# Attention and mixture of experts on one core: the products with v in two groups of six heads, the rows of a tile in one step of their own

## The chip, the cores and the metric

The kernel runs on one core of a Trainium2 chip. The metric is the device time of one execution in microseconds (us). Three runs of the kernel before took 1297.36, 1302.81 and 1301.54 us, so its median is 1301.54 us. One execution was profiled; every row below comes from it.

## The reference

For 8 batches of 448 queries with 12 heads of 64, scores are mixed over the heads before the softmax and the probabilities are mixed over the heads again after it. The attended rows (3584 tokens of 768) then go each to the best of 8 experts.

```python
scores = scale * np.matmul(q, k.transpose(0, 1, 3, 2))
scores = np.einsum('bhij,hg->bgij', scores, w_pre)
attn = np.exp(scores - max); attn /= attn.sum(-1) + 1e-9
attn = np.einsum('bhij,hg->bgij', attn, w_post)
x = np.matmul(attn, v)                    # (8, 12, 448, 64) -> (3584, 768)
expert_idx = np.argmax(x @ w_gate, axis=1)
out[token] = gate * (np.maximum(x[token] @ w1[e], 0) @ w2[e])
```

## The kernel before, in words

The attention part cuts the queries of a batch into four tiles, three of 120 queries and one of 88, so that there are 32 tiles T. A tile is worked off in steps of twenty queries (two halves of ten): six steps for a tile of 120, numbered 0 to 5 here, and five for the tile of 88, the last with one half. A batch thus has 23 steps, and the whole attention part 184.

Every step does the same softmax work on TensorE, VectorE, ScalarE and GpSimd:

- `mix` (L267, or L261 for a single half) multiplies the scores of the step with the first head mixing into two banks of PSUM, `bm`.
- `maxima` (L273, VectorE) and `powers` (L281, ScalarE) read those banks: the maximum, then the exponential and its sum. `recip` (L289, L291, VectorE) and `weigh` (L298, GpSimd) make the second mixing, divided by the sums, in the next step.
- `post` (L314) multiplies the exponentials of two steps ago with it into two banks `bp`, and `evict_p` (L332, VectorE; L326 for a single half) copies them into `pt`, the probabilities of the tile, transposed. Both banks are used by every step, so that `post` of a step needs `evict_p` of the step before.

Beside it, some steps carry work that is done once per tile. In steps 0, 2 and 4, `qk` (L239) makes the scores of four heads for a tile to come, in the four banks `bs`, and `evict_s` (L244, ScalarE) copies them out; these are the qk steps. In the others stands the product with v of the tile before: `av` (L346) for a group g of four heads (sixteen products of 64 columns, of two heads side by side, over four pieces of the keys) into the first bank of `bs`; `evict_x` (L353, VectorE) copies it into `xt`; in a later step without `qk`, `rows` (L363) turns it into rows by two products with the matrix `xg` (an identity with eight columns of the gate beside it), and `evict_r` (L370, ScalarE) copies these into `xr`. When three groups are through, `store_x` writes the rows to memory by a DMA of SyncE, and the routing follows: `choose` (L385 to L396, VectorE) finds the expert, `rank` (L404, TensorE) and `place` (L417 to L426, VectorE) its slot, `gate` (ScalarE) and `token` (L432 to L436, VectorE) the weight, and `scatter` (L442), an indirect DMA that GpSimd issues, writes slot and weight into a table.

After step 184 come the last products with v and the last routing, and then the experts: 8 times two layers of matmuls, that begin when the table and the rows have been read back.

No scheduler decides the order. `at(u, stage, ...)` puts a piece of work into step u, `ORDER` gives the order of the stages within a step, and each engine executes what it gets in that order; semaphores make it wait. For a tile of six steps the three groups of `av` of the tile before stand in steps 3, 5 and 1 of the next tile, and each group's `rows` one or two steps behind. In the tile of five steps the second group stands in step 4, which has `qk` too.

Of the kernel before, what the change touches and what calls it, by code (L numbers as in the profile page):

```python
# [8 lines left out]
F32 = mybir.dt.float32  # L9
# [10 lines left out]
B, H, S, D = 8, 12, 448, 64  # L20
# [3 lines left out]
P = 128  # L24
IT = 120
# [9 lines left out]
XG = P + NE  # L35
NTILE = B * 4
# [6 lines left out]
def attn_moe_kernel(ctx, tc, qT, kT, v, w_pre, w_post, w_gate, w1, w2, out):  # L43
    nc = tc.nc
# [291 lines left out]

    HOME = {g: bank_s[0][:, 0, :] for g in range(3)}
    SHEET = {}

    def av(T, g):  # L340
        b, it, ni = geom[T][:3]
        for p in range(2):
            for c in range(NJ):
                for r in range(2):
                    h = 4 * g + 2 * p + r
                    nc.tensor.matmul(out=HOME[g][r * D:(r + 1) * D, p * IT:p * IT + ni],  # L346
                                     lhsT=VV[b][:, c, h * D:(h + 1) * D],
                                     rhs=PT[T][:, c, h, :ni], start=(c == 0), stop=(c == NJ - 1))

    def evict_x(T, g):  # L350
        ni = geom[T][2]
        XT[T, g] = x_p.tile([P, 2, IT], F32, name="xt", bufs=3)
        nc.vector.tensor_copy(out=XT[T, g][:, :, :ni],  # L353
                              in_=HOME[g][:, :2 * IT].rearrange("p (c i) -> p c i", i=IT)[:, :, :ni])

    XR, LG, DD = {}, {}, {}

    def rows(T, g, bank):
        ni = geom[T][2]
        xt = XT.pop((T, g))  # L360
        SHEET[T, g] = bank[:, :2 * XG].rearrange("p (c x) -> p c x", x=XG)
        for c in range(2):
            nc.tensor.matmul(out=SHEET[T, g][:ni, c, :], lhsT=xt[:, c, :ni],  # L363
                             rhs=xg[:, 2 * g + c, :], start=True, stop=True)

    def evict_r(T, g):
        ni = geom[T][2]
        if g == 0:
            XR[T] = x_p.tile([IT, NPAIR, XG], F32, name="xr", bufs=2)
        nc.scalar.copy(out=XR[T][:ni, 2 * g:2 * g + 2, :], in_=SHEET.pop((T, g))[:ni])  # L370

# [10 lines left out]
    def choose(T):  # L382
        b, it, ni = geom[T][:3]
        lg = sm_p.tile([IT, NE], F32, name="lgs")
        nc.vector.reduce_sum(out=lg[:ni], in_=XR.pop(T)[:ni, :, P:XG].rearrange("p c e -> p e c"),  # L385
                             axis=AX.X)
# [102 lines left out]
    def at(u, stage, *what):  # L489
        steps.setdefault((u, stage), []).append(what)  # L490
# [11 lines left out]

    qsteps, vsteps = {}, {}
    for T in range(NTILE):
        u0, n = ustart[T], len(geom[T][3])
        for g, (dt, k) in enumerate(((2, 4), (1, 0), (1, 2))):
            if T + dt < NTILE:
                qsteps[T + dt, g] = u0 + k
        if T + 1 == NTILE:
            vsteps.update({(T - 1, g): u0 + 2 + g for g in range(3)})  # L510
            vsteps.update({(T, g): NU + 1 for g in range(3)})
            vsteps[T - 2, 2] = u0 + 1
        else:
# [3 lines left out]
    hasq = set(qsteps.values())  # L517

    def free(u):
        while u in hasq:  # L520
            u += 1
        return u

    used = {}
    for T in range(NTILE):
        b, it, ni = geom[T][:3]
        u0, n = ustart[T], len(geom[T][3])
        last = T + 1 == NTILE
        if T > 1:
# [15 lines left out]
        if last:  # L545
            continue
        for g in range(3):
            u = vsteps[T, g]
            at(u, "av", av, T, g)
            both = u in hasq  # L550
            at(u if both else u + 1, "vec_now" if both else "vec", evict_x, T, g)
            u = free(u + 1)
            bank = bank_s[1][:, used.get(u, 0), :]
            used[u] = used.get(u, 0) + 1
            at(u, "rows", rows, T, g, bank)
            at(u + 1, "evict_r", evict_r, T, g)
        at(u + 2, "store", store_x, T)
        at(u + 2, "vec", choose, T)
        u = free(u + 3) if T + 3 < NTILE else u + 2
# [35 lines left out]
    for u in range(max(u for u, _ in steps) + 1):  # L595
# [7 lines left out]
        if u == NU + 1:  # L603
            T = NTILE - 1
            HOME.update({0: bank_s[0][:, 0, :], 1: bank_s[0][:, 1, :], 2: bank_s[1][:, 0, :]})
            for g in range(3):
                av(T, g)
                evict_x(T, g)
                if g:
                    rows(T, g - 1, bank_m[g - 1])  # L610
                    evict_r(T, g - 1)
            rows(T, 2, bank_s[1][:, 1, :])
            evict_r(T, 2)
    store_x(T)
# [273 lines left out]
```

## Time and profile before

| | |
|---|---|
| median of three runs | 1301.54 us |
| the profiled execution's own time | 1301.47 us |
| its span, first to last instruction | 1299.8 us |
| TensorE busy | 1234.3 us, 95% |
| VectorE, ScalarE, GpSimd busy | 61%, 52%, 29% |
| attention part (first product with v of tile 0 to the last) | 57.6 to 731.5 us |
| one batch, step 2 of its first tile to the same step a batch later | 86.9 us |

The attention part is a little over half of the span. Durations of matmuls in the trace are modelled and overlap each other, so that what a group of matmuls costs is read from starts: from its first start to the first start of the next group.

### The profile page before, as it was taken

The page shows a single profiled execution, that of the slowest core. Times are in us where ns is not written, and L with a number is a line of the kernel's source. Part 1 is how long each engine was busy: PE and PEld are TensorE (multiplying, and loading weights), DVE is VectorE, ACT ScalarE, POOL GpSimd, SP SyncE. Part 2 cuts the span into 40 slices and gives each one's busy share as a digit, 9 for nine tenths or more (in the row PEclk, how much of TensorE's full clock was granted, in tenths as well). Part 3 has the DMA queues.
Part 4 walks back from the last instruction along what each step waited for, and adds up shares of the span by engine and source line. Part 5 has one row for each costly group of instructions (what it writes and reads, how often), then busy time and mean ns, then how long its engine had stood idle before and what let it go on. Part 6 is the DMA issues. An engine that isn't in the chain of part 4 may idle for free. (4 is left out here: it accounts for less than half of the span.)

```text
span 1299.8 us, 45032 instructions
## 1 busy us (share of the span) xinstructions
PE 1234.3 (95%) x18960; PEld 1032.0 (79%) x18960; DVE 787.9 (61%) x1995; ACT 679.0 (52%) x1468; POOL 371.8 (29%) x605
## 2 busy tenths in 40 slices
PE   6899999999999999999999469999999999999995
PEld 3677777777777777777777459898999989989995
DVE  4777887878878878788788535352434243534320
ACT  5676777767767777777674224242423242434220
POOL 4444453534434535344332120101010202010000
PEclk9999999999999999999999769999999999999998
DMA  6654746746547367566344354443444434544210
GB/s 210 195 164 142 246 123 190 210 151 204 178 136 241 125 192 213 155 201 182 130 153 134 82 178 156 145 159 122 138 140 151 131 133 142 171 135 145 87 36 33
DMA packets 133214, 200.08 MB, mean 154 GB/s; under 512 B 40002, under 2 KB 110674, under 8 KB 132996
## 3 DMA queue, kind: packets, MB, share of 16 engines
q1 hardware_dynamic: 125888, 173.08, 42.5%
q0 software_dynamic: 6064, 23.86, 5.3%
q8 instruction: 161, 2.64, 0.9%
q14 instruction: 57, 0.47, 0.1%
q10 hardware_dynamic: 1044, 0.04, 0.0%
HBM read 97.59 MB, written 23.06 MB: 93 GB/s over the span
## 5 line engine op out<-in xcount | busy, mean ns | idle before, releaser
L281 ACT ACTIVATE et<-bm,st 124x448 f32<-124x448 f32 x360 | 225.5, 632 | 139.9 <-DVE st L273 137.4
L273 DVE TENSOR_REDUCE st<-bm 124x1 f32<-124x448 f32 x360 | 208.1, 619 | 90.3 <-PE bm L267 85.7
L314 PEld LDWEIGHTS bp<-wp,et 60*64 60x64 f32 (+1 forms) x10080 | 199.8, 135 | 71.2 <-issue 48.7
L298 POOL TENSOR_SCALAR wp<-Wpost,st 124x60 f32<-124x60 f32 x360 | 151.4, 435 | 280.7 <-DVE st L291 145.2
L332 DVE COPY pt<-bp 128x480 f32<-128x480 f32 x352 | 213.8, 649 | 26.0 <-PE bp L314 25.7
L314 PE MATMUL bp<-wp,et 60*64 60x60 f32 (+1 forms) x10080 | 193.4, 219 | 1.7 <-issue 1.5
L267 PE MATMUL bm<-sb,Wquad 60*60 60x448 f32 (+3 forms) x1408 | 188.3, 566 | 5.9 <-ACT et L281 4.5
L346 PE MATMUL bs<-pt,vt 128*64 128x120 f32 (+1 forms) x3072 | 173.5, 265 | 2.5 <-DVE pt L326 1.4
L244 ACT COPY si<-bs 120x896 f32<-120x896 f32 (+1 forms) x188 | 160.8, 910 | 26.4 <-PE bs L239 25.4
L346 PEld LDWEIGHTS bs<-pt,vt 128*64 128x64 f32 x3072 | 151.5, 138 | 9.1 <-issue 2.0
L738 POOL DMA_INDIRECT out<-y,ti x30 | 30.0, 1000 | 424.3 <-ACT y L736 415.1
L708 PE MATMUL pm_h<-xh,ah 128*128 128x512 f32 (+1 forms) x384 | 146.1, 381 | 1.8 <-ACTq L767 1.5
L708 PE MATMUL pm_h<-xl,ah 128*128 128x512 f32 (+1 forms) x384 | 146.0, 380 | 0.0
L708 PE MATMUL pm_h<-xh,al 128*128 128x512 f32 (+1 forms) x384 | 144.7, 377 | 0.0
L712 DVE SCALAR_TENSOR_TENSOR hl<-pm_h,hh 128x512 fp32r<-128x512 f32 (+1 forms) x64 | 42.2, 659 | 158.1 <-ACT hh L711 158.1
L711 ACT ACTIVATE hh<-pm_h 128x512 fp32r<-128x512 f32 (+1 forms) x64 | 36.7, 573 | 174.1 <-PE pm_h L708 169.6
L729 PE MATMUL pm_y<-bh,hh 128*128 128x384 f32 x480 | 124.7, 341 | 0.0
L729 PE MATMUL pm_y<-bh,hl 128*128 128x384 f32 x480 | 122.4, 336 | 0.0
L729 PE MATMUL pm_y<-bl,hh 128*128 128x384 f32 x480 | 122.3, 336 | 0.0
L142 POOL TENSOR_TENSOR ql<-qr,qh 128x360 fp32r<-128x360 f32 (+1 forms) x78 | 69.1, 896 | 125.1 <-ACT qh L141 93.1
L736 ACT ACTIVATE y<-pm_y,tb 128x384 f32<-128x384 f32 x30 | 17.5, 582 | 146.3 <-PE pm_y L729 88.0
L239 PE MATMUL bs<-kh,qh 64*120 64x448 f32 (+1 forms) x384 | 82.0, 423 | 12.2 <-ACT kh L115 7.3
(113 smaller groups left out, 1809.2 us busy)
## 6 DMA issues: line engine op xcount, KB each, us to landing
sb<-si SPq DMA_DIRECT2D x344, 210.0 KB
wraw<-in_w SPq DMA_DIRECT2D x48, 512.0 KB
wraw<-in_w SPq DMA_DIRECT2D x64, 384.0 KB
kr<-in_kT SPq DMA_DIRECT2D x42, 224.0 KB
vt<-in_v SPq DMA_DIRECT2D x8, 1152.0 KB
qr<-in_qT SPq DMA_DIRECT2D x48, 180.0 KB
XD<-xr SPq DMA_DIRECT2D x24, 360.0 KB
vt<-in_v SPq DMA_DIRECT2D x16, 192.0 KB
```

The costliest lines, as they stand in the source:

```text
L142: (nc.vector if T == 0 else nc.gpsimd).tensor_sub(out=lo, in0=src, in1=hi.bitcast(F32))
L239: nc.tensor.matmul(out=bank_s[c % 2][:ni, r, :S], lhsT=qx[hs, c, :ni], rhs=kx[hs, :], start=(n == 0), stop=(n == 2))
L244: copy(out=SI[T][:ni, 2 * c:2 * c + 2, :], in_=bank_s[c % 2][:ni, :, :S])
L267: nc.tensor.matmul(out=bank_m[r][CUT[c], :S], lhsT=Wquad[CUT[r], CUT[c]], rhs=sb[CUT[r], c, :], start=True, stop=True)
L273: nc.vector.reduce_max(out=st[:R1, 0, c:c + 1], in_=bank_m[c][:R1, :S], axis=AX.X, negate=True)
L281: nc.scalar.activation(out=et[:R1, c, :], in_=bank_m[c][:R1, :S], func=AF.Exp, bias=st[:R1, 0, c:c + 1], scale=1.0, accum_out=st[:R1, 1, c ...
L298: nc.gpsimd.tensor_scalar(out=wp[:R1, c, :], in0=Wpost[:R1], scalar1=st[:R1, 2, c:c + 1], scalar2=None, op0=ALU.mult)
L314: nc.tensor.matmul(out=bank_p[r][col * JC:(col + 1) * JC, at_:at_ + W], lhsT=et[CUT[r], n, kg * JC:(kg + 1) * JC], rhs=wp[CUT[r], n, :], s ...
L332: nc.vector.tensor_copy(out=flat[:, :, i0 + r * IB:i0 + (r + 1) * IB] .rearrange("p x (n k) -> p x n k", k=IQ), in_=bank_p[r][:, :2 * NJ * ...
L346: nc.tensor.matmul(out=HOME[g][r * D:(r + 1) * D, p * IT:p * IT + ni], lhsT=VV[b][:, c, h * D:(h + 1) * D], rhs=PT[T][:, c, h, :ni], start ...
L708: nc.tensor.matmul(out=ph[:, :n], lhsT=wx[:, fs], rhs=xx[:, kt, :n], start=(m == 0), stop=(m == 3 * NK1 - 1))
L729: nc.tensor.matmul(out=py[g][:, :384], lhsT=hx[:, kt, ts], rhs=wx[:, g * 384:(g + 1) * 384], start=(n == 0), stop=(n == 3 * NK2 - 1))
```

## The change

The product with v of a tile is done in two groups of six heads instead of three of four. A group has 24 products instead of sixteen, and its home is three columns of pairs wide instead of two. The two groups stand in steps 3 and 5 of the next tile, each without `rows` behind it; where that tile has five steps, both stand in step 3, in two banks. The rows of the tile are made in one step of their own, step 1 of the tile after that one: six products in a row, in two banks, copied out by ScalarE in two pieces at the head of step 2. `evict_x` and `evict_r` run twice per tile, on 360 and 408 columns instead of 240 and 272. The number of products is the same.

The routing moves with it. `choose` stands in step 3 behind `evict_p` instead of at the head of a step, `rank` and `gate` stand in step 1 of the tile after, `place` in step 2, `token` behind `evict_p` of step 3, and `scatter` in step 4, behind that step's `weigh`. At the end of the attention part the same pieces stand closer.

```diff
-    def av(T, g):
+    def av(T, g, bank):
         b, it, ni = geom[T][:3]
-        for p in range(2):
+        HOME[T, g] = bank[:, :3 * IT].rearrange("p (c i) -> p c i", i=IT)[:, :, :ni]
+        for p in range(3):
             for c in range(NJ):
                 for r in range(2):
-                    h = 4 * g + 2 * p + r
+                    h = 6 * g + 2 * p + r
...
     def rows(T, g, bank):
-        for c in range(2):
+        for c in range(3):
...
-            for g, (dt, k) in enumerate(((1, 3), (1, n - 1), (2, 1))):
-                if T >= dt:
-                    vsteps[T - dt, g] = u0 + k
+        if T:
+            early = T + 1 == NTILE
+            vsteps[T - 1] = (u0 + 2, u0 + 3) if early else (u0 + 3, u0 + (5 if n > 5 else 3))
+            rsteps[T - 1] = u0 + 4 if early else u0 + n + 1
...
+        for g in range(2):
+            at(vs[g], "av", av, T, g, bank_s[0][:, g if vs[0] == vs[1] else 0, :])
+            at(vs[g] + 1, "vec", evict_x, T, g)
+            at(r, "rows", rows, T, g, bank_s[1][:, g, :])
+            at(r + 1, "evict_r", evict_r, T, g)
+        near = T + 2 - NTILE
+        at(r + 2, "store", store_x, T)
+        at(r + (1 if near == 0 else 2), "choose", choose, T)
+        u = r + 2 if near == 0 else r + 3 if near == -1 else rsteps[T + 1]
         at(u, "rank", rank, T)
         at(u, "gate", gate, T)
         at(u + 1, "vec", place, T)
-        at(u + 2, "vec", token, T)
-        at(u + 2, "scatter", scatter, T)
+        at(u + (1 if near > -2 else 2), "token", token, T)
+        at(u + (2 if near > -2 else 3), "scatter", scatter, T)
...
-             "vec_now", "qk", "evict_s", "split", "split_w")
+             "choose", "token", "qk", "evict_s", "split", "split_w")
```

TensorE, steps 1 and 3 of a tile of six steps (the difference of the two orders; `bp` is written by `post`, `bm` by `mix`, and a row with x16 stands for sixteen products in a row):

```order
 L314 MATMUL bp_106<-wp,et 64x60 x2
-L346 MATMUL bs_101<-pt,vt 64x120 x16
-L363 MATMUL bs_102<-xg,xt 120x136 x2
+L362 MATMUL bs_102<-xg,xt 120x136 x6
 L267 MATMUL bm_103<-sb_150,Wquad 64x448
...
 L314 MATMUL bp_106<-wp,et 64x60 x2
-L346 MATMUL bs_101<-pt,vt 64x120 x16
-L363 MATMUL bs_102<-xg,xt 120x136 x2
+L346 MATMUL bs_101<-pt,vt 64x120 x24
 L267 MATMUL bm_103<-sb_148,Wquad 64x448
```

Each of these steps had a group of `av` and a group of `rows` between `post` and the next `mix`; now it has one of the two, and a longer one.

TensorE, steps 3 and 4 of the tile of five steps:

```order
-L346 MATMUL bs_101<-pt,vt 64x120 x16
-L363 MATMUL bs_102<-xg,xt 120x136 x2
+L346 MATMUL bs_101<-pt,vt 64x120 x48
 L261 MATMUL bm_103<-sb_150,Wpre 124x448
...
 L314 MATMUL bp_106<-wp,et 64x60 x2
-L346 MATMUL bs_101<-pt,vt 64x120 x16
 L239 MATMUL bs_101<-kh,qh 120x448 x2
```

All 48 products of the tile before now stand in step 3, and step 4 has `qk` directly behind `post`.

VectorE, the end of a step and the head of the next around `choose`, before:

```order
L332 COPY pt<-bp_106 128x48x10
L289 TENSOR_SCALAR st<-st 124x2
L291 RECIPROCAL st<-st 124x2
L385 TENSOR_REDUCE lgs<-xr 120x8
...
L396 TENSOR_SCALAR sc<-m_2110 120x1
L273 TENSOR_REDUCE st<-bm_103 124x1
```

and now (steps 3 and 4):

```order
L332 COPY pt<-bp_106 128x48x10
L384 TENSOR_REDUCE lgs<-xr 120x8
...
L395 TENSOR_SCALAR sc<-m_2916 120x1
L431 TENSOR_SCALAR sc<-sc 88x1
L434 RECIPROCAL tg<-sc 88x1
L435 COPY tg<-tokid 88x1
L289 TENSOR_SCALAR st<-st 124x2
L291 RECIPROCAL st<-st 124x2
L353 COPY xt<-bs_101 128x360
L273 TENSOR_REDUCE st<-bm_103 124x1
```

The six lines of `choose` and the three of `token` stand ahead of `recip` and `evict_x` of the next step, where `choose` stood behind `recip`.

## Rows read from the trace of the kernel before

**Rows 1.** The page: busy time of each engine, and TensorE's granted clock in forty slices of the span (tenths of full speed).

```profile
PE 1234.3 (95%) x18960; PEld 1032.0 (79%) x18960; DVE 787.9 (61%) x1995; ACT 679.0 (52%) x1468; POOL 371.8 (29%) x605
PEclk9999999999999999999999769999999999999998
```

**Rows 2.** Waits of TensorE between 40 and 860 us, two of eleven: line and what it waited for, us in total, times, longest.

```profile
PE pm_x L661 <- DMA xs<-XD,tcl: 16.1, 1, 16.1
...
PE bs L239 <- DVE st L289: 3.6, 7, 0.5
```

**Rows 3.** Two stretches of one batch (four tiles) each: length, then busy us of PE, PEld, DVE, ACT and POOL with their instructions, granted clock, share of the DMA engines, GB/s.

```profile
205.27:292.41 87.14, 86.42 (x2023) 67.41 (x2022) 70.45 (x210) 63.45 (x150) 38.63 (x66) 1.00 0.58 178
...
379.33:466.22 86.89, 86.31 (x2024) 67.46 (x2023) 70.48 (x210) 63.44 (x150) 38.67 (x66) 1.00 0.57 181
```

**Rows 4.** TensorE in order of time, around three groups of `av` and `rows`: start us, length us, line, operation, records (one product has two).

```profile
202.37 1.86 PE L346 MATMUL bs<-pt,vt 128*64 128x120 f32 x32
204.16 1.19 PE L363 MATMUL bs<-xg,xt 128*120 128x136 f32 x8
205.27 0.98 PE L267 MATMUL bm<-sb,Wquad 64*64 64x448 f32 x8
206.08 0.99 PE L314 MATMUL bp<-wp,et 64*64 64x60 f32 x56
206.99 0.47 PE L239 MATMUL bs<-kh,qh 64*120 64x448 f32 x2
...
210.21 1.77 PE L346 MATMUL bs<-pt,vt 128*64 128x88 f32 x32
211.91 0.72 PE L363 MATMUL bs<-xg,xt 128*120 128x136 f32 x4
212.56 0.98 PE L267 MATMUL bm<-sb,Wquad 64*64 64x448 f32 x8
...
224.79 1.43 PE L346 MATMUL bs<-pt,vt 128*64 128x88 f32 x32
226.15 0.70 PE L363 MATMUL bs<-xg,xt 128*88 128x136 f32 x4
```

**Rows 5.** TensorE in step 4 of the tile of five steps: `av` and, behind it, `qk` (in brackets the idle time before it, and what ended that).

```profile
106.80 1.86 PE L346 MATMUL bs<-pt,vt 128*64 128x120 f32 x32
109.17 0.46 PE L239 MATMUL bs<-kh,qh 64*120 64x448 f32 x2 [0.51 <-DVE st L289]
```

**Rows 6.** The turn from a qk step to a step 5 (which begins with the row of PE): VectorE, and `mix` of TensorE.

```profile
302.11 1.21 DVE L332 COPY pt<-bp 128x480 f32<-128x480 f32 x2
303.24 0.16 DVE L289 TENSOR_SCALAR st<-st 124x2 f32<-124x2 f32 x1
...
303.51 0.22 DVE L385 TENSOR_REDUCE lgs<-xr 120x8 f32<-120x48 f32 x1
...
304.64 1.15 DVE L273 TENSOR_REDUCE st<-bm 124x1 f32<-124x448 f32 x2
...
302.82 1.29 PE L267 MATMUL bm<-sb,Wquad 64*64 64x448 f32 x8
```

**Rows 7.** All engines in a step 3, which begins with the first row: the scatter and what stands beside it.

```profile
295.55 1.06 PE L267 MATMUL bm<-sb,Wquad 64*64 64x448 f32 x8
295.73 0.16 DVE L289 TENSOR_SCALAR st<-st 124x2 f32<-124x2 f32 x1
...
296.00 0.13 DVE L432 TENSOR_SCALAR sc<-sc 120x1 f32<-120x1 f32 x1
...
296.25 0.13 DVE L436 COPY tg<-tokid 120x1 int32<-120x1 int32 x1
296.28 0.84 POOL L298 TENSOR_SCALAR wp<-Wpost,st 124x60 f32<-124x60 f32 x2 [2.18 <-DVE sc L432]
...
297.29 1.05 POOL L442 DMA_INDIRECT TB<-tg,di  x1 [0.18 <-DVE st L273]
297.34 0.96 PEld L346 LDWEIGHTS bs<-pt,vt 128*64 128x64 f32 x24
...
298.55 0.38 PEld L346 LDWEIGHTS bs<-pt,vt 128*64 128x64 f32 x8 [0.25 <-issue]
...
298.62 1.22 DVE L332 COPY pt<-bp 128x480 f32<-128x480 f32 x2 [0.80 <-PE bp L314]
```

**Rows 8.** TensorE and GpSimd at the end of the attention part, where a scatter stands beside `post`.

```profile
705.86 0.85 PE L314 MATMUL bp<-wp,et 64*64 64x60 f32 x43
...
706.35 1.04 POOL L442 DMA_INDIRECT TB<-tg,di  x1 [0.18 <-issue]
...
707.58 0.39 PE L314 MATMUL bp<-wp,et 60*64 60x60 f32 x9 [0.39 <-issue]
707.89 1.86 PE L346 MATMUL bs<-pt,vt 128*64 128x120 f32 x32
```

**Rows 9.** The copy of a group's products by VectorE, between 60 and 700 us: count, busy us, mean ns of one, idle before.

```profile
L353 DVE COPY xt<-bs 128x240 f32<-128x240 f32 x67 | 26.4, 393 | 4.2 <-PE bs L346 4.0
```

**Rows 10.** ScalarE at the turn from step 1 to step 2.

```profile
291.23 0.82 ACT L141 CAST qh<-qr 128x360 fp32r<-128x360 f32 x1
292.52 0.68 ACT L370 COPY xr<-bs 120x272 f32<-120x272 f32 x2 [0.47 <-PE bs L363]
294.24 0.64 ACT L281 ACTIVATE et<-bm,st 124x448 f32<-124x448 f32 x1 [1.05 <-DVE st L273]
```

More of the change, by code (lines that the diff above doesn't have):

```diff
@@ L335, in evict_p @@
                 in_=bank_p[r][:, :2 * NJ * W].rearrange("p (n x k) -> p x n k", n=2, k=IQ))
-    HOME = {g: bank_s[0][:, 0, :] for g in range(3)}
-    SHEET = {}
-    def av(T, g):
+    HOME, SHEET = {}, {}
+    def av(T, g, bank):
         b, it, ni = geom[T][:3]
-        for p in range(2):
+        HOME[T, g] = bank[:, :3 * IT].rearrange("p (c i) -> p c i", i=IT)[:, :, :ni]
+        for p in range(3):
             for c in range(NJ):
                 for r in range(2):
-                    h = 4 * g + 2 * p + r
-                    nc.tensor.matmul(out=HOME[g][r * D:(r + 1) * D, p * IT:p * IT + ni],
+                    h = 6 * g + 2 * p + r
+                    nc.tensor.matmul(out=HOME[T, g][r * D:(r + 1) * D, p, :],
                                      lhsT=VV[b][:, c, h * D:(h + 1) * D],
@@ L351, in evict_x @@
         ni = geom[T][2]
-        XT[T, g] = x_p.tile([P, 2, IT], F32, name="xt", bufs=3)
-        nc.vector.tensor_copy(out=XT[T, g][:, :, :ni],
-                              in_=HOME[g][:, :2 * IT].rearrange("p (c i) -> p c i", i=IT)[:, :, :ni])
+        XT[T, g] = x_p.tile([P, 3, IT], F32, name="xt", bufs=2)
+        nc.vector.tensor_copy(out=XT[T, g][:, :, :ni], in_=HOME.pop((T, g)))
     XR, LG, DD = {}, {}, {}
@@ L360, in rows @@
         xt = XT.pop((T, g))
-        SHEET[T, g] = bank[:, :2 * XG].rearrange("p (c x) -> p c x", x=XG)
-        for c in range(2):
-            nc.tensor.matmul(out=SHEET[T, g][:ni, c, :], lhsT=xt[:, c, :ni],
-                             rhs=xg[:, 2 * g + c, :], start=True, stop=True)
+        SHEET[T, g] = bank[:, :3 * XG].rearrange("p (c x) -> p c x", x=XG)[:ni]
+        for c in range(3):
+            nc.tensor.matmul(out=SHEET[T, g][:, c, :], lhsT=xt[:, c, :ni],
+                             rhs=xg[:, 3 * g + c, :], start=True, stop=True)
     def evict_r(T, g):
@@ L369, in evict_r @@
             XR[T] = x_p.tile([IT, NPAIR, XG], F32, name="xr", bufs=2)
-        nc.scalar.copy(out=XR[T][:ni, 2 * g:2 * g + 2, :], in_=SHEET.pop((T, g))[:ni])
+        nc.scalar.copy(out=XR[T][:ni, 3 * g:3 * g + 3, :], in_=SHEET.pop((T, g)))
     def store_x(T):
@@ L384, in choose @@
         lg = sm_p.tile([IT, NE], F32, name="lgs")
-        nc.vector.reduce_sum(out=lg[:ni], in_=XR.pop(T)[:ni, :, P:XG].rearrange("p c e -> p e c"),
+        nc.vector.reduce_sum(out=lg[:ni], in_=XR[T][:ni, :, P:XG].rearrange("p c e -> p e c"),
                              axis=AX.X)
@@ L500, in attn_moe_kernel @@
         at(u + PL, "evict_p", evict_p, T, s)
-    qsteps, vsteps = {}, {}
+    qsteps, vsteps, rsteps = {}, {}, {}
     for T in range(NTILE):
@@ L527, in attn_moe_kernel @@
         u0, n = ustart[T], len(geom[T][3])
-        last = T + 1 == NTILE
         if T > 1:
@@ L544, in attn_moe_kernel @@
                 at(U - 15 + 2 * c, "early", split_k, b + 1, c)
-        if last:
+        if T + 1 == NTILE:
             continue
[L547 to L559, printed above, removed]
+        vs, r = vsteps[T], rsteps[T]
+        for g in range(2):
[7 more added lines that the diff above has]
+        u = r + 2 if near == 0 else r + 3 if near == -1 else rsteps[T + 1]
         at(u, "rank", rank, T)
@@ L604, in attn_moe_kernel @@
             T = NTILE - 1
-            HOME.update({0: bank_s[0][:, 0, :], 1: bank_s[0][:, 1, :], 2: bank_s[1][:, 0, :]})
-            for g in range(3):
-                av(T, g)
+            for g in range(2):
+                av(T, g, bank_s[g][:, 0, :])
                 evict_x(T, g)
[L609 to L613, printed above, removed]
+            for g in range(2):
+                rows(T, g, bank_m[g])
+                evict_r(T, g)
     store_x(T)
```

11 lines of the change are left out of this document (removed).

## The prediction, made before the changed kernel was run

> **What bounds the kernel now.** I read the page first, for the busy shares: TensorE is busy for 95% of the span, the other engines for 29 to 61%, and the clock is granted nearly everywhere but at the turn to the experts [rows 1]. Second the waits of TensorE, to see whether the busy share hides a wait. Beside one wait of 16.1 us for the first rows of the experts, none of them sums to more than a few microseconds; the one that this change touches is `qk` waiting seven times for about 0.5 us on VectorE [rows 2]. Third the stretches of one batch: 86.9 to 87.1 us, TensorE busy for all but 0.6 of them, VectorE for 70.5 and ScalarE for 63.5, at full clock [rows 3]. So in the attention part TensorE is the pacer, and what a group of products costs is the distance from its first start to the next group's [rows 4]. What changes those distances changes the time; what VectorE and ScalarE save is worth nothing as long as they keep up. The experts are untouched.
>
> **The change part by part.** The number of products stays; what changes is how often TensorE goes from one kind to another.
>
> *Rows.* A group of two products takes 211.91 to 212.56 = 0.65 us, one of four takes 204.16 to 205.27 = 1.11 [rows 4]. A further two cost 0.46, so 0.19 of each group is its turn in and out. A batch has twelve groups of two, of which two stand together (the row with x8): eleven turns. Four groups of six are left: 7 x 0.19 = 1.33 us less per batch.
>
> *Products with v.* Sixteen of them take 202.37 to 204.16 = 1.79 us with 120 columns and 224.79 to 226.15 = 1.36 with 88 [rows 4]. They run as eight pairs, so 32 columns are 0.43 / 8 = 0.053 us, 120 columns 0.20, and eight pairs 1.60: again 0.19 for the turn. A batch goes from twelve turns to seven (two groups for three tiles; in the tile of five steps both stand in a row): 5 x 0.19 = 0.95 us less. What this rests on is that `rows` behind `post`, which the trace does not show, has the same turn as behind `av`. It could be none or, at most, the 0.19 of `av` on top of its own; from the rows I take them alike.
>
> *The step with both av and qk.* There `av` to `qk` is 106.80 to 109.17 = 2.37 us instead of 1.79: `qk` needs the bank that `evict_x` still empties [rows 5]. Now both groups stand in step 3 and a `mix` and a `post` come before `qk`: 0.58 us less, once a batch.
>
> *The scatter.* In step 3 the indirect DMA occupies GpSimd from 297.29 for 1.05 us [rows 7]. In that time TensorE's weight loads go on for 24 and then stop until 298.55, and VectorE's copy of `post`'s result, with nothing else to wait for, starts at 298.62, 0.80 us late: TensorE's signals and then TensorE itself are held until about 0.2 us behind the scatter's end. Its price is seen in `av` of 88 columns: 210.21 to 211.91 = 1.70 against 1.36 [rows 4]. It goes from this place: 0.34 us less, once a batch; with 120 columns the same hold costs TensorE under 0.1, and I count nothing. The Trainium skill ("SBUF — State Buffer", section "SBUF: two separate sides") says that contention arises only at the port that GpSimd and VectorE share, and that TensorE and ScalarE never wait on anyone. Here that disagrees with the rows of the scatter, and the rows decide. By the page the 0.34 would have another cause and stay, and the sum would come out 2.6 us later.
>
> *Where the scatter goes.* To step 4, which has `qk`, and there it must not meet `post`. I work out its start from step 3's `mix`. `post` ends 0.80 + 1.01 after it, and `evict_p` begins some 0.4 later, at 2.2. Then VectorE runs `evict_p` (302.11 to 303.24, 1.13), `choose` (303.51 to 304.64, 1.13) and `token` (0.38) [rows 6, 7]; from L289 to the start of `weigh` is 0.55, from there to the scatter 1.01 [rows 7]. That makes 2.2 + 1.13 + 1.13 + 0.38 + 0.55 + 1.01 = 6.4. The next `mix` starts at 0.80 + 1.01 + 2.59 (24 products: 1.79 + four pairs x 0.20) = 4.4, so the scatter falls 2.0 us into step 4. `post` ends there at 0.81 + 0.91 = 1.72 (205.27, 206.08, 206.99 [rows 4]). It clears `post` by 0.3 us and lies beside `qk`, which has few instructions and no one waiting soon. I take nothing for it. In the tile of five steps it lies beside the long `av`, with 88 columns deeper in `qk`.
>
> *VectorE's queue.* `choose` and `token`, 1.5 us, now stand ahead of `recip`, `evict_x` and the next `maxima`, and `weigh`, ScalarE's exponential and the next `mix` wait behind them. Behind a step 3 of 4.4 us the queue is free at 2.2 + 1.13 + 1.13 + 0.38 + 0.27 = 5.1, and with 0.51 for `evict_x` (0.39 for 240 columns [rows 9] and an estimated 0.12 for 120 more, the VectorE instruction's remainder taken as fixed) at 5.6: 1.2 into step 4, about when `mix` is done. Behind a step 3 of 88 columns (0.80 + 1.01 + 1.95 = 3.8) it is 1.9. A maximum that began 304.64 - 302.82 = 1.8 late already stood in each batch, and there `mix` took 1.29 where 1.06 is usual [rows 6, 7]. One such place goes and one comes: nothing.
>
> *Copies.* VectorE saves 3 x 0.39 - 2 x 0.51 = 0.15 us per tile, beside TensorE. ScalarE's two copies at the head of step 2 grow from 0.68 to some 0.9 us; the exponential behind them waited 1.05 us for VectorE [rows 10], which covers it. SyncE's queue gets the same transfers, the store one step later; nothing reads it before the experts.
>
> *Sum.* 1.33 + 0.95 + 0.58 + 0.34 = 3.2 us per batch. 31 tiles have their work inside the steps, 7.75 batches: 24.8 us. I give back 2 us for waits in the shorter steps that no row prices (bounds: 0, and 1.6 per batch, half of the gain). The end of the attention part has the same pieces in other order; I take zero, within 3 us either way. The profiled execution took 1301.47 us, practically the median of 1301.54: 1301.5 - 24.8 + 2 = 1279.
>
> **The rivals.**
>
> *VectorE and ScalarE become the bound.* For: VectorE would be busy 70 us of 83.7, and its queue has 1.5 us more in one lump. Against: the maximum of most steps waits for `mix`, not the other way round, and the lump stands behind the longest step. If TensorE waits 0.4 us in four steps of a batch, 1.6 x 7.75 = 12 us are lost: 1291.
>
> *The turns do not go.* If `rows` behind `post` and `av` ahead of `mix` bring turns as dear as those that left, only 0.58 + 0.34 remain, 7 us: 1294, within what can be told from no change. For: no such neighbours in most steps. Against: a group of four takes 1.11, not 1.30.
>
> *The scatter meets post: slower.* At one place it did: `post` from 705.86 to 707.89 took 2.03 us, where 0.91 to 1.01 is usual, a full 1.0 more, because `post` is the densest string of instructions [rows 8]. If the scatter starts more than about 0.6 us earlier in step 4 than I work out, it falls on `post` in each tile: 31 x 1.0 = 31 us, 1310. At 0.3 earlier only the signals of `post` are held, `evict_p` is 0.8 late and the next `post` waits some 0.4: in two tiles of four 6 us, 1285. For: the margin is 0.3. Against: every delay on VectorE moves it later, away from `post`.
>
> **How the numbers follow.** The forecast 0.62, VectorE 0.16, the turns 0.12, the scatter 0.10. The forecast's own range is 1270 to 1287: 3 us better at the end and 6 for the small waits that now stretch single steps and may vanish, 8 worse for half a margin. Adding VectorE and the turns reaches 1294, which leaves the scatter at its worst and a little at the low end out: 1267 to 1294. Half a percent, 6.5 us, is about what can be told from no change. Faster by more than that (below 1295) are the forecast and most of the two middle cases: 0.79. Within it: 0.12. Slower: 0.09.
>
> **What would show it.** Right: a batch of 83.5 to 84 us, `rows` of six at 1.58 us, `av` of 24 at 2.59 (1.95 with 88 columns), no wait of `qk` on VectorE, the scatter starting about 2 us into step 4 and `post` there still 0.92. Wrong: `post` of step 4 above 1.3 us, waits of `mix` on ScalarE in steps 4 and 5, or a `rows` group well above 1.6.

## The result and the profile after

The changed kernel takes 1310.72 us (median of 15 runs, 1302.39 to 1319.89), the kernel before 1302.0 (1296.56 to 1304.52): ratio 1.0072, 95% interval 1.0044 to 1.0099. It is slower by 0.7%, and lies above the whole range that was forecast. The profiled execution's span is 1310.6 us.

The groups cost what the prediction says. TensorE around a `rows` of six products and an `av` of 24, in a stretch without waits:

```profile
253.48 1.63 PE L362 MATMUL bs<-xg,xt 128*120 128x136 f32 x12
255.04 0.98 PE L267 MATMUL bm<-sb,Wquad 64*64 64x448 f32 x8
...
259.97 2.68 PE L346 MATMUL bs<-pt,vt 128*64 128x120 f32 x48
262.58 0.60 PE L267 MATMUL bm<-sb,Wquad 64*64 64x448 f32 x4
```

253.48 to 255.04 is 1.56 us (forecast 1.58), 259.97 to 262.58 is 2.61 (forecast 2.59). But the batch did not get shorter. One batch of the new kernel, as in [rows 3], and three of TensorE's waits, here over the whole span (line and what it waited for, us in total, times, longest):

```profile
199.46:287.29 87.83, 84.90 (x2025) 66.49 (x2023) 71.49 (x205) 61.52 (x146) 38.60 (x65) 1.00 0.61 178
```

```profile
PE bp L314 <- issue: 14.1, 8, 3.3
...
PE bs L239 <- DVE xt L353: 4.2, 7, 0.7
PE bs L346 <- issue: 3.1, 4, 1.5
```

TensorE works 1.5 us less than in [rows 3] and waits 2.9 us where it waited 0.7. `post` (L314) stands still for up to 3.3 us at a time and no engine is named for it: "issue" means that nothing in the profile released it. The wait of `qk` (L239) on VectorE has not gone; its releaser is now `evict_x` (L353). This is a stop of `post`, in step 4 of a batch's second tile:

```profile
238.27 0.98 PE L267 MATMUL bm<-sb,Wquad 64*64 64x448 f32 x8
239.07 0.80 PE L314 MATMUL bp<-wp,et 64*64 64x60 f32 x41
241.49 0.46 PE L314 MATMUL bp<-wp,et 64*64 64x60 f32 x15 [1.62 <-issue]
241.87 0.44 PE L239 MATMUL bs<-kh,qh 64*88 64x448 f32 x2
```

It comes in the second tile of six batches in a row, lasts 1.6 to 3.5 us from the start of the last instruction before it to the start of the next, and is missing in the last batch, which loads no v. (The first batch loads v too, and has stops of 1.25 and 1.77 us at other instructions.) Often another follows in the next `av`. Counted in the trace's list of TensorE (semaphore instructions included), the six stops stand behind instructions 5568, 9664, 13760, 17856, 21952 and 26048: 4096 apart, and each a multiple of 64. A batch of this program has 4090 instructions, so a stop that belonged to the program would come back every 4090. These come every 4096, and move three records on in `post` with each batch: behind the 38th, 41st, 44th, 47th, 50th and 53rd. The first and the last of the six:

```profile
151.29 0.75 PE L314 MATMUL bp<-wp,et 64*64 64x60 f32 x38
153.74 0.46 PE L314 MATMUL bp<-wp,et 60*64 60x60 f32 x17 [1.70 <-issue]
...
593.63 0.97 PE L314 MATMUL bp<-wp,et 64*64 64x60 f32 x53
596.86 0.32 PE L314 MATMUL bp<-wp,et 60*64 60x60 f32 x3 [2.25 <-issue]
```

What stops TensorE thus goes by the count of its instructions, and not by what they compute. The instructions themselves come by DMA, in packets of 16 KB. The DMA queues from 238.6 to 239.9, at the stop (packets, MB, share of the engines' time):

```profile
q1 hardware_dynamic: 103, 0.26, 90.2%
q8 instruction: 1, 0.02, 4.7%
```

One instruction packet moves from 238.81 to 239.78; TensorE goes on 1.71 us after its end. In the eleven stops above 0.45 us between 90 and 700 us that distance is 1.4 to 1.7 us. There are 161 such packets in the run, and through the attention part one for each 256 instructions. The earliest of them start 1.0 to 1.1 us after instruction 256n + 128 has run, so I take that for the request; the stops stand at 256n + 448, so I take it that the packet is needed there. TensorE then has 320 instructions in hand, 5 to 10 us of this program. At 9664 it had 5.73 us in hand; the packet started only 4.89 us behind the request. What stood ahead of it is in SyncE's queue, now and then in the kernel before (one row per run of issues):

```profile
232.13 0.81 SPq L374 DMA_DIRECT2D XD<-xr  x1
233.00 0.55 SPq L149 DMA_DIRECT2D vt<-in_v  x1
233.60 2.85 SPq L153 DMA_DIRECT2D vt<-in_v  x2
```

```profile
226.26 0.39 SPq L149 DMA_DIRECT2D vt<-in_v  x1
```

The request falls at 233.92, 0.92 us behind the issue of the 1152 KB of v. In the kernel before, v was issued at 226.26, 4.08 us ahead of the request of the same number. Now the store of the rows (L374) stands in the same step ahead of it and waits for ScalarE's copy of the rows, which ends at 232.11.

The second loss is on VectorE. Step 4 of a first tile, beginning at 216.10, VectorE and then GpSimd:

```profile
216.57 0.90 DVE L393 TENSOR_SCALAR ohb<-iota,sc 120x8 bf16<-120x8 f32 x1
217.38 0.14 DVE L395 TENSOR_SCALAR sc<-m 120x1 f32<-120x1 f32 x1
...
218.03 0.41 DVE L353 COPY xt<-bs 128x264 f32<-128x264 f32 x1
```

```profile
216.30 1.15 POOL L142 TENSOR_TENSOR ql<-qr,qh 128x360 fp32r<-128x360 f32 x1 [2.40 <-ACT qh L141]
...
219.32 1.04 POOL L441 DMA_INDIRECT TB<-tg,di  x1 [0.18 <-issue]
```

`choose` (to L395) and `token` stand ahead of `evict_x` (L353), and L393 takes 0.90 us beside GpSimd's `ql`, to just behind its end, where it takes 0.23 to 0.29 in the kernel before and in e3, without `ql` beside it. This agrees with the Trainium skill ("SBUF — State Buffer", section "SBUF: two separate sides"): VectorE and GpSimd share a port. `qk` then waits for its bank, and the next step starts late.

The loss has three candidates: the store ahead of v (F, by the fetch), `choose` and `token` at the end of the step (L), and the scatter in step 4, either by its work on GpSimd (S) or by its own transfers (X).

### The profile page after: what moved, and what is told of

The parts are those of the page before. It is cut to its first block, busy times and chain, and to the rows that moved or that the text cites. A ratio compares the mean times of both kernels' runs of the same rounds, so it can differ in the third digit from the quotient of the medians.

```text
span 1310.6 us, 44937 instructions
## 1 busy us (share of the span) xinstructions
PE 1226.2 (94%) x18960; PEld 1027.9 (78%) x18960; DVE 794.3 (61%) x1963; ACT 664.7 (51%) x1436; POOL 371.7 (28%) x605
## 5 line engine op out<-in xcount | busy, mean ns | idle before, releaser
L314 PEld LDWEIGHTS bp<-wp,et 60*64 60x64 f32 (+1 forms) x10080 | 200.6, 135 | 88.4 <-issue 68.1
L314 PE MATMUL bp<-wp,et 60*64 60x60 f32 (+1 forms) x10080 | 198.3, 219 | 16.1 <-issue 14.1
L267 PE MATMUL bm<-sb,Wquad 60*60 60x448 f32 (+3 forms) x1408 | 192.5, 567 | 8.2 <-ACT et L281 5.4
L346 PE MATMUL bs<-pt,vt 128*64 128x120 f32 (+1 forms) x3072 | 164.0, 264 | 5.1 <-issue 3.1
L239 PE MATMUL bs<-kh,qh 64*120 64x448 f32 (+1 forms) x384 | 82.6, 427 | 13.0 <-ACT kh L115 7.3
L267 PEld LDWEIGHTS bm<-sb,Wquad 64*64 64x64 f32 (+3 forms) x1408 | 44.7, 130 | 61.0 <-issue 35.7
```

The lines of the kernel that those rows point to most:

```text
L239: nc.tensor.matmul(out=bank_s[c % 2][:ni, r, :S], lhsT=qx[hs, c, :ni], rhs=kx[hs, :], start=(n == 0), stop=(n == 2))
L267: nc.tensor.matmul(out=bank_m[r][CUT[c], :S], lhsT=Wquad[CUT[r], CUT[c]], rhs=sb[CUT[r], c, :], start=True, stop=True)
L314: nc.tensor.matmul(out=bank_p[r][col * JC:(col + 1) * JC, at_:at_ + W], lhsT=et[CUT[r], n, kg * JC:(kg + 1) * JC], rhs=wp[CUT[r], n, :], s ...
L346: nc.tensor.matmul(out=HOME[T, g][r * D:(r + 1) * D, p, :], lhsT=VV[b][:, c, h * D:(h + 1) * D], rhs=PT[T][:, c, h, :ni], start=(c == 0), ...
```

## The experiments

In the table, "seven batches" runs from the `mix` of the single half in tile 3 (its last step) to the one in tile 31. "Stops" adds up, between 90 and 700 us, the distances above 0.25 us from an instruction at a multiple of 64 to the next; up to 2 us of each sum are ordinary waits that fall on such a place by chance. Both are of the one profiled execution. Ratios are to the kernel before on the same chip; e1 to e4, e5 to e8, e9 to e12 and e13 to e16 ran on a chip each, so that the other two columns compare over chips too.

```
                                  ratio   95%               seven batches   stops
before                            1                              609.4       2.6
the change                        1.0072  1.0044 - 1.0099        617.1      18.5
e1  loads ahead of the store      1.0000  0.996  - 1.004         605.9      12.7
e2  128 instructions shifted      1.0017  0.9984 - 1.0049        610.9      12.8
e3  routing at its old places     0.9941  0.9913 - 0.9969        604.1      16.6
e4  e1 and e3 together            0.9843  0.9767 - 0.9919        589.9       6.7
e12 e4 again                      0.9898  0.9864 - 0.9932        595.8      10.7
e9  e4, 64 instructions shifted   0.9881  0.9824 - 0.9937        594.5      10.5
e5  e4, v in four pieces          1.0050  1.0011 - 1.0088        620.0      20.1
e6  e4, v two steps later         1.0022  0.9982 - 1.0063        607.2       3.2
e10 e4, choose at the step's end  0.9931  0.9898 - 0.9965        607.5      15.0
e8  e4, scatter in step 4         0.9985  0.9954 - 1.0016        624.9      30.8
e11 e8 without any scatter        0.9723  0.9666 - 0.9780        593.3      10.9
e7  before, 160 shifted           1.0059  1.0035 - 1.0082        621.9      10.9
```

### e1: the loads ahead of the store

```diff
-    ORDER = ("relayout", "store", "load", "fetch", "mix", ...
+    ORDER = ("relayout", "load", "store", "fetch", "mix", ...
```

> Edit: in each step the loads go into SyncE's queue ahead of the store of the routed rows; nothing else moves. Theory F (TensorE's instructions are fetched over the same DMA engines; in the second tile of a batch the fetch is asked for less than 1 us behind the 1152 KB load of v, which the store held back to 233.00, and lands after TensorE has used up what it had): v is issued some 4 to 6 us earlier, in the step before, the fetch that follows starts about 3.4 us behind its request instead of 4.9, and the stops of 1.6 to 3.5 us inside post of the second tile's fourth step (record 9664 and every 4096th behind it) go: 17 us in all, about 1294 (1289 to 1300). Rival S (the scatter's descriptor work on GpSimd stops TensorE there, since it lies beside each of these post groups): nothing changes, 1311 within 4. Rival W (post waits for data or a semaphore that the load of v delays): the stops move or shrink too, but need not lie at a multiple of 64 records.

No difference from the kernel before, so 0.7% better than the change. SyncE's queue in the same batch (this run is some 9 us ahead of the change here, so times are to be read against the request, now at 224.78):

```profile
220.95 1.90 SPq L149 DMA_DIRECT2D vt<-in_v  x1
...
225.52 0.89 SPq L374 DMA_DIRECT2D XD<-xr  x1
```

The request at 9664 now stands 3.83 us behind v, and its stop is 1.42 us instead of 1.84; others went down more. The stops moved with the transfer, which S alone does not allow, but they fell by 6 us, not by 17. New stops stand one request earlier, where the request falls 1.5 to 1.7 us ahead of v and the packet still starts 5 to 6 us late in three of six batches.

### e2: TensorE's instructions shifted by 128

```diff
+    for _ in range(64):
+        nc.tensor.matmul(out=bank_m[0][:, :8], lhsT=tri, rhs=ones[:, :8], start=True, stop=True)
     load_v(0)
```

> Edit: 64 products of 8 columns are put into the prologue of TensorE, which adds 128 records (64 weight loads, 64 products) ahead of everything and moves no transfer and no other engine's work; their results are overwritten. Theory F: the places at which TensorE needs the next 16 KB of instructions shift by 128 records against the program: the request that stood 0.9 us behind the load of v now stands at about 231.5 us, 1.5 us ahead of it, and the next one 4 us behind it. The stops of 1.6 to 3.5 us at the second tile's fourth step go, what is left lies at other instructions of the program, again at multiples of 64 records counted with the padding: about 1296 (1290 to 1303), the padding itself at most 4 us in the prologue. Rivals S (scatter) and W (data): the stops stay at the same instruction of the program, 41 products into post: 1311 to 1315.

The stops at 5568, 9664 and so on are gone from `post` of step 4. In the batch shown step 4 runs through, and a short stop stands in step 5, behind instruction 9920 with the padding counted:

```profile
232.76 0.99 PE L314 MATMUL bp<-wp,et 64*64 64x60 f32 x56
...
235.86 0.63 PE L314 MATMUL bp<-wp,et 64*64 64x60 f32 x28
236.90 0.68 PE L314 MATMUL bp<-wp,et 60*64 60x60 f32 x28 [0.40 <-issue]
```

No transfer, wait or scatter was moved against the program, so only the places of the requests can have done this: it is the fetch. The sum fell only to 12.8 us, for two large stops came at 21952 and 26048 (3.05 and 2.35 us, in `av` of step 3): there the request falls 0.9 and 1.2 us ahead of v, and the packets started 6.6 and 6.0 us late.

### e3 and e4: the routing at its old places, and both

```diff
-        at(r + (1 if near == 0 else 2), "choose", choose, T)
+        at(r + (1 if near == 0 else 2), "choose" if near == 0 else "vec", choose, T)
...
-        at(u + (1 if near > -2 else 2), "token", token, T)
-        at(u + (2 if near > -2 else 3), "scatter", scatter, T)
+        at(u + (1 if near > -2 else 2), "token" if near > -2 else "vec", token, T)
+        at(u + 2, "scatter", scatter, T)
```

> Edit: choose goes back to the head of its step on VectorE, token to the head of step 3 and the scatter into step 3, as in the kernel before; the two groups of six, their rows and the store stay. Theory F: TensorE's program and the transfers are the same, so the stops in the second tile's fourth step stay (17 us in all), with no scatter beside them. What goes are the wait of qk for evict_x in the first tile (0.67 to 0.82 per batch) and the late mix and post of the following steps (0.54, twice a batch); the scatter beside av of 88 columns costs 0.34 again: 1.5 us less per batch, 12 us: about 1299 (1294 to 1304). Rival S: the stops go too, for the scatter now lies beside av: 1311 - 12 - 17 = 1282.

> Edit: the loads ahead of the store, and the routing at its old places (the two edits together). Theory F: both losses go, 17 and 12 us: about 1282 (1276 to 1290), faster than the kernel before by 1.5%. Rival S: the order of the transfers adds nothing, the same time as with the routing alone, 1282 as well, but then e3 shows 1282 too.

e3: no scatter lies near, and `post` stops at the same records. At 9664:

```profile
232.09 0.80 PE L314 MATMUL bp<-wp,et 64*64 64x60 f32 x41
233.84 0.46 PE L314 MATMUL bp<-wp,et 64*64 64x60 f32 x15 [0.96 <-issue]
```

That rules S out as the cause of these stops. What went is the routing's loss: with the stops taken off, the seven batches take 587.5 us instead of 598.6, 1.6 a batch. e4, two batches, the second with a stop:

```profile
188.74:272.32 83.58, 83.57 (x2024) 66.58 (x2022) 68.87 (x205) 61.50 (x146) 38.44 (x65) 1.00 0.60 187
272.33:357.10 84.77, 83.78 (x2025) 66.45 (x2023) 68.96 (x205) 61.62 (x146) 38.42 (x65) 1.00 0.60 184
```

83.58 us is the batch that was forecast (83.5 to 84), and 1277.45 us about the time (1279), in four runs. Measured again, less of it stood:

> The kernel with the loads ahead of the store and the routing at its old places once more, unchanged, in more rounds: 0.984 to the kernel before (0.979 to 0.989) if the first measurement holds.

0.9898, just above what was expected, with stops of 10.7 us instead of 6.7 from the same program, on another chip. How late a fetch is differs between the two profiled executions: the request for 17856 was served 3.0 us late in one and 5.3 in the other.

### e7: the stops brought into the kernel before

The padding of e2 with 80 products, in the kernel before.

> Edit, on the kernel before, nothing of the change: 80 products of 8 columns in the prologue, 160 records of TensorE, which move the places where it asks for instructions against the program; no transfer and no other engine's work moves. From the trace of before, a request then falls 0.5 to 1.4 us behind the load of v in each batch, with 5.6 to 6.1 us of work in hand, and the next one 5.1 to 5.5 us behind it with 7.0 to 7.4. Theory F: stops of 1 to 2.5 us at the first of them in six batches, up to 0.8 at the second: 9 to 18 us slower than before, ratio 1.007 to 1.014. Rivals S and W, and anything else that the change itself brought: no difference but the padding, 0 to 4 us, ratio 1.000 to 1.003.

Slower by 0.6%, just under the expected band and clear of the 0 to 0.3% of the padding. In six batches TensorE stops at instructions 5568, 9664 and so on, 8.6 us in all, now in `av` (four), `rows` and ahead of `mix`:

```profile
236.13 1.45 PE L346 MATMUL bs<-pt,vt 128*64 128x120 f32 x23
238.92 0.67 PE L346 MATMUL bs<-pt,vt 128*64 128x120 f32 x9 [1.34 <-issue]
```

So the stops need nothing of the change: a request close to the load of v, here from 0.3 us ahead of it to 1.4 us behind, with 5.8 to 6.1 us in hand in five of the six, is enough.

### e5, e6 and e9: three ways to spare the last stops

```diff
-            at(u0 + 9, "load", load_v, b + 1)
+            for part in range(NJ):                              # e5
+                at(u0 + 9 + part, "load", load_v, b + 1, part)
+            at(u0 + 11, "load", load_v, b + 1)                  # e6
```

The diff shows both runs, each marked; in e5 `load_v` issues one piece of v at a time. e9 has the padding of e2 with 32 products.

> Edit, on the kernel with the loads ahead of the store and the routing at its old places: the load of v goes out in four pieces (three of 384 KB, one of 192 KB), one per step, instead of 1152 and 192 KB in one step. TensorE's program is the same. Theory F: the stops at records 5568, 13760, 17856, 21952 and 26048 (0.3 to 1.6 us, 5.6 together) go, because a request of TensorE now stands behind at most 384 KB: the fetch starts within 3.2 us of its request there, and no stop is above 0.3: 1272 (1268 to 1277), ratio to the kernel before 0.980. Rival Q (what delays the fetch is the number of transfers in the queue or the relayouts, not the size of the load of v): the stops stay, 1277.

> Edit, on the same base: the load of v stays whole and goes two steps later. Theory F: the request for records 9664 and every 4096th from it (5.1 to 6.0 us of work in hand) then lies some 4 us ahead of the load and its fetch starts 1 to 2 us behind it; the next one (record 9920, 7.0 to 7.6 us in hand) takes the delay instead, 4 to 6 us, of which it bears about 5: stops of 0 to 1 us there, none at the old place: 1273 to 1279. Rival Q: the stops stay at record 9664 and its like, 1277.

> Edit, on the kernel with the loads ahead of the store and the routing at its old places: 32 products of 8 columns in TensorE's prologue, 64 records, nothing else. From that kernel's trace the request nearest to the load of v then falls 2.0 to 2.1 us behind it with 7.1 us of work in hand, instead of 3.5 to 4.6 us with 5.1 to 6.1. Theory F: at 4 to 5 us of delay the fetch is in time, the stops of 0.3 to 1.6 us go or fall under 0.4: 5 us less, ratio to the kernel before 0.980 where 0.984 stands without the shift (0.977 to 0.983). If what stops TensorE there is not the fetch, nothing changes: 0.984 to 0.986.

All three missed. e5's stops moved on to other requests (5824, 13504, 18112 and others) and grew, to 5.98 us at 18112: spread over four steps, the pieces seem to meet more requests. That a stop is set by the size of the one transfer ahead is refuted; the old places are nearly free (one stop of 0.5 us), so Q is too. e6 took the fetch's stops away but for one of 1.25 us, as F says, and lost more elsewhere: the loads of q and the relayouts now queue behind v. Step 2 of the third tile, where ScalarE waits for q, takes 5.3 us in e6 and 3.1 in e4. ScalarE's longest wait on a load in one batch of e6:

```profile
ACT qh L141 <- DMA qr<-in_qT: 3.0, 1, 3.0
```

e9 gained nothing: at 2 us behind v packets started 4.3 to 5.7 us late, and the next request, 7 us behind v, 4.1 to 6.8.

### e8, e11 and e10: scatter and choose apart

e8 puts `token` and `scatter` back where the change has them, `choose` stays at the head; e11 also leaves out the scatter; e10 puts only `choose` back.

> Edit, on the kernel with both edits (1277.5): token goes back to the end of step 3 and the scatter to step 4, as in the change, while choose stays at the head of step 3. VectorE reaches token 1.1 us earlier than in the change, so the scatter starts 0.8 to 1.4 us behind step 4's mix, when post runs, instead of 1.9 to 3.2. If post is held as in the one place of before (2.03 us instead of 0.92 to 1.01): 28 times 1.0, about 1305. If only the signals of post are held and the following copy and post come late: 0.3 to 0.5 per tile, about 1288 to 1291. If the scatter costs TensorE nothing and the late steps of the change came from VectorE alone: 1277.5 within 3.

> Edit, on the kernel of run e8 (choose at the head of step 3, token at the end, scatter in step 4; 1301): the scatter is left out in every tile, so the table of rows stays empty and the experts' rows are not the reference's; token and everything else stay. Theory X (the scatter's own transfers, 1.4 to 3 us behind it, slow the loads of q that go out in the same step, and everything behind them in the queues, TensorE's fetch with them): the fetches asked 1.5 us ahead of the load of v start within 1.5 us as in the kernel with both edits, instead of 6; the stops fall from 32 us to under 8, the attention part is 24 us shorter: 1277 or, without the scatter's hold of TensorE at the end, a few us less. If it is token's place on VectorE that does it, the stops stay: 1300.

> Edit, on the kernel with both edits: choose alone goes back to the end of its step, where the change has it; token and scatter stay at their old places. Theory L (the first tile's late steps come from VectorE: choose stands ahead of evict_x there and its last comparison takes 0.90 instead of 0.23 us beside GpSimd's subtraction ql, so that qk waits for the bank): the wait of 0.7 to 0.8 us of qk in the first tile of each batch returns, the mix held by the scatter (0.54) doesn't: 5 to 7 us slower than that kernel, about 1283, ratio 0.988. If the scatter alone makes the late steps: 1277, ratio 0.984.

e8 tested only in part what it was made for. The scatter waits for `weigh` ahead of it on GpSimd: in the first and third tile it starts 2.5 to 2.8 us into step 4, beside `qk`, and in the tile of five steps beside the long `av`. Only in the second tile it meets `post`, in four batches, 0.4 to 0.6 us into step 4. There `post` is held by 0.4 to 0.6 us, at no multiple of 64, 2 us in all:

```profile
326.76 1.04 POOL L441 DMA_INDIRECT TB<-tg,di  x1 [0.18 <-issue]
327.12 0.74 PE L314 MATMUL bp<-wp,et 64*64 64x60 f32 x37
328.25 0.38 PE L314 MATMUL bp<-wp,et 60*64 60x60 f32 x7 [0.39 <-issue]
```

What it showed beside that is X. Its seven batches take 35 us more than e4's, 24 of them stops; without the scatter (e11) 20 us of stops go again and 32 of the time. (e11's experts are 10 us shorter too, their table of rows being empty.) The DMA engines while a load of q runs, in e4 (the quickest of its seven) and then in e8 (the last two numbers are the DMA engines' busy share and GB/s):

```profile
210.50:212.50 2.00, 2.00 (x56) 1.90 (x54) 1.88 (x5) 1.34 (x4) 0.00 (x0) 1.00 0.85 224
```

```profile
213.50:217.50 4.00, 4.00 (x118) 3.32 (x116) 3.18 (x9) 1.57 (x5) 0.83 (x2) 1.00 0.75 91
```

Busy, but 91 GB/s instead of 224. The load's 768 packets of 352 bytes take 41 to 65 ns each on average in the seven loads of e8, and 22 to 27 in e4: a few dozen last up to 3.5 us, where none in e4 lasts above 0.35. From first to last packet the seven loads of this shape between 60 and 690 us take 2.1 to 3.1 us in the kernel before, 3.4 to 5.4 in the change, 1.8 to 3.9 in e4, 3.7 to 5.2 in e8 and 1.8 to 2.5 in e11. Scatter packets lie in all seven in the change and e8, in none in before and e4. Every request 1.5 to 1.7 us ahead of v is served 5.8 to 6.9 us late in e8 and 1.2 to 2.8 in e4. That the slow load brings this, by what is queued behind it, is argued and not shown: without the scatter (e11) three of the six are still 4.9 to 5.8 us late.

e10 came out the other way round than L said: the longer step 5 of the first tile (4.2 us instead of 3.7) returned without the scatter, so it comes from `choose`; the wait of `qk` mostly did not. By the steps `choose` makes 1.0 of the routing's 1.6 us a batch (0.1 and 0.5 in steps 4 and 5 of the first tile, 0.3 in step 5 of the third). e10's stops were higher than e4's too, for which I have no reason; its first batch took 91.9 us, 4.6 of them two stops.

### e13 to e16: no load of v inside the batches

```diff
-                                     lhsT=VV[b][:, c, h * D:(h + 1) * D],
+                                     lhsT=VV[0][:, c, h * D:(h + 1) * D],
...
-            at(u0 + 9, "load", load_v, b + 1)
```

> Edit, on the kernel of the change: v is loaded once and the later batches use the first batch's, so the output is not the reference's from the second batch on; the six loads of v inside the batches are left out, nothing else. Theory F (the fetch is late because it stands behind the load of v): the stops at multiples of 64 records fall from 18.5 us to under 2, each batch takes 85.0 (83.5 and 1.5 for the routing's new places): 1291 to 1295, ratio 0.995. If relayouts, loads of q or the scatter alone make the fetch late: stops of more than 5 us stay, 1298 or more.

> The same edit on the kernel before. Theory F: its stops are 2.6 us in all, so it gains at most 3 us: ratio 0.997 to 1.000, and the change without the loads of v is faster than this one by 87.0 - 85.0 = 2 us a batch, 14 us. If the load slows other things too (copies, relayouts), before gains more than 5 us.

> The same edit on the kernel with the loads ahead of the store and the routing at its old places (ratio 0.984 and 0.990 in two measurements, stops of 7 and 11 us): stops under 2 us, each batch 83.5: ratio 0.978 to 0.981, 1272 to 1277. If the stops there have another cause: 0.984 to 0.990.

> The same edit on the kernel of run e8 (scatter at the end of step 4, stops of 31 us, ratio 0.9985). If the scatter only pushes the transfers in front of the load together so that the request meets it: the stops fall under 3 us, 1273 to 1280, ratio 0.98. If the scatter's transfers delay the fetch by themselves: more than 8 us of stops stay and the ratio is 0.985 or more.

All four leave out the seven loads of v inside the batches. With the first batch's v the tokens spread differently over the experts, whose part takes 811 us instead of 584; so only the seven batches can be compared.

```
                     with the loads of v      without
                     batches   stops       batches   stops
before      (e16)     609.4     2.6         603.1     2.7
the change  (e13)     617.1    18.5         610.0     8.0
e4 and e12  (e14)   589.9 595.8 6.7 10.7    587.8     4.2
e8          (e15)     624.9    30.8         585.9     2.6
```

In e8 the load of v is needed for the stops: the scatter alone delays no fetch enough. In the change it is not all: without v, four batches take the expected 84.5 to 85.3 us, three 89 to 91.5. Stops stand there at other places, beside or just behind loads of q that took 4.7 to 6.6 us; one of them, 1.85 us, is at no multiple of 64, so the fetch does not explain it. The stops that were expected to fall under 2 us fell to 8.0 (e13) and 4.2 (e14). The kernel before gains 6.3 us without a change in its stops, which F does not explain. The ratios, all 1.15 to 1.17, say nothing on this.

## Why the prediction was wrong, point by point

- **Turns, right.** `rows` of six 1.56 us, `av` of 24 2.61 and, with 88 columns, 1.97 (1.95). The 3.2 us per batch are in e4: 83.58 in place of 86.9 to 87.1.
- **The step with both av and qk, right**, in the tile of five steps. In step 4 of each first tile a new wait of `qk` for `evict_x` came, 0.5 to 0.7 us.
- **The scatter's 0.34, right in size, wrong in what brings it.** In e4 the scatter stands beside `av` of 88 columns as before, and that `av` takes 1.97 with it (e4) and without it (e11): a hold does not show there. The move was not needed for this gain.
- **Where the scatter goes: "I take nothing for it", failed.** In the tiles of six steps it started 1.8 to 3.3 us into step 4 and in the tile of five steps 0.1 to 0.5 us into the last step, and it held `post` only in two of the tiles of five steps, by 0.4 us, so the rival feared here did not come. What the step left out are the scatter's own transfers, which now meet the load of q: 3.4 to 5.4 us instead of 2.1 to 3.1. With the loads ahead of the store that brings 20 us of stops (e8 against e11); in the change as it stands it can be only a small part, for without it 16.6 of the 18.5 us stay (e3).
- **VectorE's queue: "One such place goes and one comes: nothing", failed.** The step summed lengths from places without GpSimd's `ql` beside them (0.23 us for the comparison that took 0.90). And it compared the queue with `mix` and the next maximum, where `qk` waits for `evict_x`: its own sum had that end 1.9 us into step 4 of the first tile, behind `post`'s end at 1.72; it began at 1.93. `choose`, `token` and the scatter at their new places cost 1.6 us a batch, 12 us in all (e3 against the change, without stops), of which `choose` alone is 1.0 a batch (e10).
- **Copies: "SyncE's queue gets the same transfers, the store one step later; nothing reads it before the experts", failed.** It asked who reads the store, not what is queued behind it. The store now holds the load of v back by 3 us against TensorE's requests (4.08 to 0.92 us ahead of the one at 9664), close in front of one, and the stops are 16 us more than before. Of these the loads ahead of the store take 6 away beside the new routing (e1) and 6 to 10 beside the old (e3 against e4 and e12). The 4 to 8 us that stay in e4 and e12 are not the store's. The prediction has no term for them: the new order of products moves the requests too, and those just behind v find TensorE with 5.1 to 6.1 us in hand in e4, 5.6 to 6.5 in the kernel before. That such a move alone can bring stops is shown by e7; what it costs here was not measured alone.
- **Sum.** 12 and 16 of the 32 us between 1279 and the result. Some 4 more are lost ahead of the seven batches (their first `mix` starts at 109.2 us, 105.0 before), where the stops of 1.25 and 1.77 us stand; this part was not taken apart. The slower outcome was given 0.09, by a mechanism that did not act in this kernel; in e8, where it did, it took 0.4 to 0.6 us a time and not 1.0.

The first of the three marks named as wrong, "`post` of step 4 above 1.3 us", appeared (up to 4.5 us), for a reason that was not among the rivals.

## What to carry to other kernels

A long string of unrolled products lives on its instruction fetch: list every transfer that a step moves with what stands behind it in its queue, and look for "issue" stops at multiples of 64 instructions, which drift against the program from one round to the next, before explaining a wait by data. When a group is made longer, put the small work that hung on it back to its old places first and measure the two apart; here the groups gave 1 to 1.6%, and the new places of the routing and the store took about 2% away.

## What the runs showed of the hardware that was not expected

- TensorE can run out of instructions. The Trainium skill ("Runtime: NRT & Kernel Launch", section "Instruction fetch mechanics") has blocks of 16 KB, which the packets here confirm, and calls the fetch mostly hidden; here it stopped TensorE for up to 3.5 us in the change and 5.98 in e5.
- A request 0.9 to 1.7 us ahead of the load of v was served in 1.1 to 1.5 us in some batches and in 5 to 6.6 in others of the same run (e1, e2, e12), in a few between. What decides it stays open, and with it whether the spread of the change's times, 1302 to 1320, comes from there.
- A load of short packets takes 3.7 to 5.2 us with a scatter of 120 rows beside it and 1.8 to 2.5 without (e8 and e11), while the DMA engines read as busy.
